# Attention and gated feed-forward in one kernel: values of four heads in a row, products begun block by block, one transpose step moved ahead of the first tile, and another pace of attention beside tile 0

## The chip, the cores and the metric

The kernel runs on one core of a Trainium2 chip. The metric is the device time of one execution in microseconds (us); several executions are timed and the median is given. One execution was also taken with the hardware profiler, and all durations below come from it.

## What is computed

There are 8 batches of 8 heads with 576 positions and 64 numbers per head. Each head gets causal attention with a decay bias; the heads of a batch, side by side, are the rows of a matrix with 4608 rows and 512 columns; a gated feed-forward follows.

```python
scores = q @ k.T / sqrt(64)
cum    = cumsum(max(s, 0))
scores = where(causal, -1e9, scores + min(-(cum_i - cum_j), 0))
x      = softmax(scores) @ v            # 8 x 8 heads -> 4608 x 512
g      = x @ w_gate                     # 512 -> 1536
out    = (g * sigmoid(g) * (x @ w_val)) @ w_out
```

## The kernel before, in words

**Attention.** Heads are numbered 0 to 63 over all batches; four heads make a group, `hb` 0 to 15. For each group, k and q are loaded as float32 (`load_one`, L140), cast to bfloat16 (`cast_one`, L246) and turned so that the head's 64 numbers lie along the partitions. For the first groups TensorE does the turning: `prep_one(hb, i)` issues 5 or 4 transposes into a PSUM bank (`pe_transpose`, L287) for one part of k or q (i = 0 and 2 are the two parts of k, 1 and 3 those of q), then copies the bank's upper half into the tile `kq` at once and leaves the copy of the lower half in a list, `seconds` (`pe_out`, L314 on ScalarE, L316 on VectorE). From group 5 on it goes through memory: the cast tile is stored (`scratch`, L260, `ks` and `qs`), read back by a DMA transpose (`transposes`, L270, `pk` and `pq`) and copied into `kq` by VectorE (`split`, L274).

A head's scores are computed in four chunks (`score_piece`): products into a bank (L359; heads 0 to 7 add a mask by a product, L353), the exponential on ScalarE into the tile `pt` (L369), and for later heads the causal mask on GpSimd (L374, L379). `av_piece` multiplies by the values (15 products with 65 columns, L396), `av_out` divides on VectorE (L412, L413, tile `ot`). For the first two batches, `x_pe` turns a pair of heads by five transposes (L446) and copies them into `XT`, the input of the feed-forward (L451 on ScalarE, L453 on VectorE); later pairs go through memory.

**Feed-forward.** It works on nine tiles of 512 rows. `gate_value` goes over 12 blocks of 128 columns; each block has a gate item and a value item of four products with 512 columns (`products`, L631, one product for each of the four pairs of heads in a batch). The gate is followed by a tanh on ScalarE (L645, `th`) and a VectorE operation (L647, `pp`), the value by another (L658, `ht`). Tiles 0 and 1 then take `down_plain` (L681): 48 products, in tile 0 sorted so that four banks stay open. The other tiles use `down_seven` (L730).

**The order.** All instructions stand in the order in which the code issues them, engine by engine. PSUM has eight banks; `take` hands out the one that was given back longest ago in this order, so that a bank's next user waits for its last reader on the chip.

The heads 0 to 7 come first, in a prologue written out by hand. Before the loop over tiles it begins the first three gate products of tile 0 with three of their four blocks, which need the first three pairs of heads:

```python
        values(4)
        x_pe(0, nc.vector)
        values(5)
        x_pe(1, nc.vector)
        values(6)
        x_pe(2, nc.scalar)
        prep_one(2, 0)
```

In the loop, each item of the feed-forward (`ffn_items`) has a cost `n` in units of one gate or value item. Behind each item, the copies in `seconds` are issued, then what `hook` holds for that `n` (for tile 0: the other three `prep_one` of group 2, the casts of group 3, the loads of `w_out`), and then `pump` issues attention pieces up to a position that grows evenly with `n`: tile 0 takes the attention from position 8.0 (head 8) to 17.65, beginning at n = 5 and ending at n = 36; gate and value end at n = 24. `PREP_AT` puts the turning of group 3 between pieces of heads 8 to 11, `side` and `side_v` put casts, stores and loads beside others: the cast of k 5 on GpSimd stands behind the second score chunk of head 15. `do_later` issues the `split` copies.

**Queues.** Loads of the first q, k and v and all transposes by DMA are issued on SP's queue, the weights and the loads of groups 1 to 3 on GpSimd's queue, in the order of the code. "k 2" and "q 2" below are k and q of group 2.

Of the kernel before, what the change touches and what calls it, by code (L numbers as in the profile page):

```python
# [19 lines left out]
def kernel(  # L20
# [11 lines left out]
    nc = tc.nc  # L32
# [13 lines left out]
    TT = 512  # L46
# [53 lines left out]
    XT = const.tile([128, 4, XR], BF16)  # L100
# [9 lines left out]
    with tc.manual_schedule():  # L110
# [9 lines left out]
        def take():  # L120
            b = min(bank, key=lambda x: released[x])
            assert released[b] < OPEN
            released[b] = OPEN
            return b
# [11 lines left out]
        def load_one(hb, name, rs=(0, NR), eng=nc.sync):  # L136
            b, g = divmod(hb, 2)
            if rs[0] == 0:
                loaded[name, hb] = raw.tile([128, NR, J, D], FP32, tag="raw" + name, name="raw" + name)
            eng.dma_start(  # L140
                loaded[name, hb][:, rs[0] : rs[1], :, :].rearrange("x r j d -> x r (j d)"),
                SRC[name][0][b, g * HB + 2 * rs[0] : g * HB + 2 * rs[1], :, :].rearrange(
                    "(r e) (p j) d -> (e p) r (j d)", e=2, j=J
                ),
            )
# [16 lines left out]
        def cast_v(b, c, eng):  # L162
            n = 128 if c < 4 else TAIL
            dst, src_t = VT[b % 2][0:n, c, :, 0:D], loaded["v", b][0:n, c, :, :]
            if eng is nc.scalar:
                nc.scalar.copy(dst, src_t)
            else:
                eng.tensor_copy(dst, src_t)
# [152 lines left out]
        def w_load(kind, j, h=None):  # L321
            dst = {"g": WG, "v": WV, "o": WO}[kind][j]
            if kind == "o":
                src_ap = moe_w_out[j * WKO * 128 : (j + 1) * WKO * 128, :].rearrange(
                    "(c p) n -> p c n", p=128
                )
            else:
                w = moe_w_gate if kind == "g" else moe_w_val
                lo, hi = (0, WCH) if h is None else (h * WCH // 2, (h + 1) * WCH // 2)
                src_ap = w[:, j * WCH + lo : j * WCH + hi].rearrange("(c p) n -> p c n", p=128)  # L330
                dst = dst[:, :, lo:hi]
            nc.gpsimd.dma_start(dst, src_ap)
# [106 lines left out]
        def x_pe(pr, eng=None):  # L439
            b, r = divmod(pr, H // 2)  # L440
            ot = ots.pop(pr)
            bs = take()
            ps = view16(bs, S)
            for c in range(NCH):
                n = 128 if c < 4 else TAIL
                nc.tensor.transpose(  # L446
                    ps[:, c * 128 : c * 128 + n], ot[0:n, c, :], ident[0:n, 0:n]
                )
            for lo, hi, at in x_parts(b):
                if eng is nc.scalar:  # L450
                    nc.scalar.copy(XT[:, r, at : at + hi - lo], ps[:, lo:hi])  # L451
                else:
                    nc.vector.tensor_copy(XT[:, r, at : at + hi - lo], ps[:, lo:hi])  # L453
            give(bs)
# [69 lines left out]

        seconds = []

        def prep_one(hb, i):
            g, nm = divmod(i, 2)
            nm = ("k", "q")[nm]
            pe_transpose(hb, nm, g)  # L530
            eng = nc.scalar if nm == "k" else nc.vector
            pe_out(hb, nm, g, 0, eng)
            seconds.append(lambda: pe_out(hb, nm, g, 1, eng))

# [12 lines left out]
        def attn_items():  # L547
            for kk in range(H, BH + 2):
                h, step = divmod(kk, HB)
                if kk < BH:  # L550
                    if step == 0:
                        do_later(NR * 2)
                    if step == 1 and 3 < h + 1 < NPE:
                        cast_one(h + 1, "k", nc.gpsimd)
                        cast_one(h + 1, "q", nc.gpsimd)
                    if step == 2 and 3 < h + 1 < NPE:
                        aug(h + 1, GP4)
                    for ci in range(4):
                        score_piece(kk, ci)
                        side(h, step, ci)  # L560
                        side_v(h, step, ci)
                        yield kk + 0.1 + ci / 8
                        if (step, ci) in PREP_AT.get(h, ()):
                            prep_one(h + 1, PREP_AT[h][step, ci])
                            yield kk + 0.1 + ci / 8
                for x in X_AT.get(kk, (kk - 2,)):
                    if x % 2 == 1 and H <= x < BH:
                        if x < XB * H:
                            x_pe(x // 2)
                            yield kk + 0.5  # L570
                        else:
                            x_in(x // 2)
                for p in AV_AT.get(kk, (kk - 1,)):
                    if H <= p < BH:
                        av_piece(p, (0, 1, 2))
                        yield kk + 0.6
                        av_piece(p, (3,))
                        yield kk + 0.7
                        av_piece(p, (4,))
                        av_out(p)  # L580
                        if p >= XB * H and p % 2 == 1:
                            x_out(p // 2)
                        yield kk + 0.8
# [35 lines left out]

        begun = {}  # L620

        def products(kind, ft, xt, cs=range(4)):
            j, f0 = divmod(ft * 128, WCH)
            w = (WG if kind == "g" else WV)[j]
            if (kind, ft) in begun:
                bs, c0 = begun.pop((kind, ft))
                cs = range(c0, 4)
            else:
                bs = take()
            for c in cs:  # L630
                nc.tensor.matmul(  # L631
                    view(bs, TT), w[:, c, f0 : f0 + 128], xt[:, c, :],
                    start=(c == 0), stop=(c == 3),
                )
            if cs[-1] < 3:
                begun[kind, ft] = bs, cs[-1] + 1
            return bs

        def gate_value(tt, hps, sus):
# [255 lines left out]
        def values(*hs):  # L895
            for h in hs:
                av_piece(h, range(NCH))
                av_out(h)
# [20 lines left out]
            cast_v(0, c, nc.gpsimd)  # L919
        load_one(2, "k", eng=nc.gpsimd)  # L920
        cast_v(0, 3, nc.gpsimd)
        w_load("v", 0, 0)
        load_one(2, "q", eng=nc.gpsimd)
        w_load("v", 0, 1)
        for nm in ("g", "v"):
            w_load(nm, 1, 0)
# [25 lines left out]
        load_v(1, range(5))  # L952
        load_qk(4)
        load_qk(5)
        values(4)
        x_pe(0, nc.vector)
        values(5)
        x_pe(1, nc.vector)
        values(6)
        x_pe(2, nc.scalar)  # L960
        prep_one(2, 0)
        while seconds:
            seconds.pop(0)()
        values(7)
        products("g", 0, XT[:, :, 0:TT], range(3))
        x_pe(3, nc.vector)
        for ft in (1, 2):
            products("g", ft, XT[:, :, 0:TT], range(3))
        give(spare)
        first_sbuf.close()  # L970
        PTP[0] = ctx.enter_context(tc.tile_pool(name="later", bufs=1))
# [4 lines left out]
        def pump(upto):  # L976
            while state["pos"] < upto:
                try:
                    state["pos"] = next(at)
                except StopIteration:  # L980
                    state["pos"] = 1e9
# [6 lines left out]
        def at_item(n, f, *args):  # L988
            hook[n].append(lambda: f(*args))

        for n, i in ((1, 2), (2, 1), (3, 3)):
            at_item(n, prep_one, 2, i)
        at_item(7, cast_one, 3, "k", nc.gpsimd)
        at_item(8, cast_one, 3, "q", nc.gpsimd)
        at_item(10, w_load, "o", 0)
# [1 line left out]
        for tt in range(NTT):  # L997
            lo = H * (tt + 1) + LAGS[tt]
            hi = min(H * (tt + 2) + LAGS[tt + 1], BH + 2)
            span = 36 if tt < FIRST7 else 34.5  # L1000
            if hi == BH + 2:
                span = 30
            n0 = 5 if tt == 0 else 0
            n = 0
            todo = {FIRST7 - 1: W_SUMS, FIRST7: W_DIFFS}.get(tt, [])
            if tt == FIRST7:
                for _ in range(3):
                    weight_op(*todo.pop(0))
            for i, cost in enumerate(ffn_items(tt)):
                n += cost  # L1010
                if todo and (i >= 24 if tt < FIRST7 else i % 2 == 1):
                    weight_op(*todo.pop(0))
                if i >= 2 * NFT or i % (2 if tt == 1 else 4) == 1:
                    do_later(1)
                while seconds:
                    seconds.pop(0)()
                for f in hook.pop(n, ()):
                    f()
                pump(lo + (hi - lo) * min(1.0, max(0, n - n0) / (span - n0)))
        pump(1e9)  # L1020


# [28 lines left out]
```

## Time and profile before

| what | value |
|---|---|
| median of 5 runs | 378.45 us (377.62 to 379.64) |
| the profiled execution | 377.62 us |
| its span, first to last instruction | 375.3 us |
| granted TensorE clock, mean | 1.000 |
| TensorE busy | 365.4 us, 97% |
| VectorE, ScalarE, GpSimd busy | 77%, 64%, 57% |
| DMA | 64.23 MB, 171 GB/s on average |

A line of the timeline gives the start, the busy time, engine, code line, operation, output<-input with the shape and the number of instructions merged into it; in brackets, how long the engine was idle just before and what ended that. A line of the chain gives start, length, engine and code line. TensorE's instructions overlap, so their busy times may not be added; the starts tell when the next could go. Times in the text count from the start of the span.

### The profile page before, as it was taken

How to read it: one execution, taken by the hardware profiler on the slowest of the kernel's cores; microseconds unless marked ns; L12 is line 12 of the kernel's file. 1: busy time of each engine (PE TensorE's matmuls, PEld its weight loads, DVE VectorE, ACT ScalarE, POOL GpSimd, SP SyncE). 2: the span in 40 equal slices, each digit the busy share in tenths (PEclk: the TensorE clock that was granted, in tenths of full speed). 3: DMA queues.
4: the chain of work that ended last, by engine and by line, in shares of the span. 5: the costliest groups of instructions: out<-in, count | busy, mean ns of one | idle time of the engine just before them, and what ended most of it. 6: DMA issues, size and time to landing. Idle time of an engine off the chain costs nothing.

```text
span 375.3 us, 8798 instructions
## 1 busy us (share of the span) xinstructions
PE 365.4 (97%) x3300; PEld 231.9 (62%) x3300; DVE 289.9 (77%) x579; ACT 239.9 (64%) x470; POOL 212.9 (57%) x325
## 2 busy tenths in 40 slices
PE   8898999999999999999999999999999999999995
PEld 7574556555555556855685559655865585476464
DVE  7867687367995999679976997599858867975984
ACT  8885967588976887578757876687465523323321
POOL 8965665765465647494649555955675416315320
PEclk9999999999999999999999999999999999999999
DMA  7899999899599997896769775996132103002003
GB/s 238 190 260 254 218 269 263 204 324 243 162 187 276 249 255 216 168 277 216 215 157 262 190 173 166 233 199 152 39 109 73 35 19 128 2 0 90 24 0 114
DMA packets 97146, 64.23 MB, mean 171 GB/s; under 512 B 77232, under 2 KB 82736, under 8 KB 97104
## 3 DMA queue, kind: packets, MB, share of 16 engines
q1 hardware_dynamic: 84976, 41.46, 47.0%
q0 software_dynamic: 12128, 22.21, 22.5%
q8 instruction: 26, 0.43, 0.5%
q14 instruction: 16, 0.13, 0.1%
HBM read 37.90 MB, written 19.86 MB: 154 GB/s over the span
## 4 chain that ended last, share of the span: by engine, by line
PE 87%; DMA 3%; DVE 3%; POOL 2%; ACT 2%; issue 1%; DVEq 0%; POOLq 0%; ACTq 0%
PE bank L631 47%; PE bank L730 17%; PE bank L359 10%; PE bank L396 8%; PE bank L681 3%; DMA pk<-ks 2%; ACT pt L369 1%; DVE kq L316 1%; DMA kq<-HL 1%; DVE pp L647 1%; DMA ks<-ck 1%; DVE ht L658 1%; PE bank L446 1%; PE bank L353 1%; PE bank L287 1%
## 5 line engine op out<-in xcount | busy, mean ns | idle before, releaser
L369 ACT ACTIVATE pt<-bank 128x512 bf16<-128x512 f32 (+1 forms) x256 | 120.2, 509 | 30.9 <-PE bank L359 22.6
L631 PE MATMUL bank<-XT,wv 128*128 128x512 bf16 x432 | 110.9, 379 | 0.6 <-DVE ht L658 0.4
L631 PE MATMUL bank<-XT,wg 128*128 128x512 bf16 x432 | 111.2, 379 | 0.1
L645 ACT ACTIVATE th<-bank 128x512 bf16<-128x512 f32 x108 | 64.7, 599 | 57.9 <-PE bank L631 52.7
L647 DVE SCALAR_TENSOR_TENSOR pp<-th,bank 128x512 bf16<-128x512 bf16 x108 | 73.7, 683 | 21.3 <-ACT th L645 20.8
L658 DVE SCALAR_TENSOR_TENSOR ht<-pp,bank 128x512 bf16<-128x512 bf16 x108 | 74.1, 686 | 10.5 <-PE bank L631 0.4
L359 PE MATMUL bank<-kq 128*128 128x128 bf16 (+4 forms) x576 | 75.3, 240 | 2.0 <-DVE kq L316 1.4
L667 POOL TENSOR_TENSOR ht<-ht 128x512 bf16<-128x512 bf16 x35 | 40.4, 1155 | 52.3 <-DVE su L665 52.2
L359 PEld LDWEIGHTS <-kq 128*128 128x128 bf16 x576 | 45.8, 98 | 32.6 <-issue 3.5
L631 PEld LDWEIGHTS <-wv 128*128 128x128 bf16 x432 | 38.4, 98 | 36.5 <-issue 1.3
L631 PEld LDWEIGHTS <-wg 128*128 128x128 bf16 x432 | 38.3, 98 | 34.1
L374 POOL TENSOR_SCALAR_AFFINE_SELECT pt<-pt 128x512 bf16<-128x512 bf16 x56 | 36.8, 658 | 27.9 <-ACT pt L369 23.0
L396 PEld LDWEIGHTS <-pt 128*128 128x128 bf16 x960 | 41.5, 98 | 16.8
L396 PE MATMUL bank<-vt,pt 128*128 128x65 bf16 x960 | 46.6, 194 | 0.0
L430 POOL DMA_DIRECT2D xs<-ot x24 | 21.7, 904 | 29.6 <-DVE ot L413 27.3
L730 PEld LDWEIGHTS <-ht 128*128 128x128 bf16 x336 | 31.2, 98 | 4.3
L413 DVE TENSOR_TENSOR ot<-bank,rc 128x320 bf16<-128x320 f32 x64 | 31.5, 492 | 2.2
L183 POOL DMA_DIRECT2D kq<-HL x48 | 28.9, 604 | 0.0
L681 PE MATMUL bank<-wo,ht 128*128 128x512 bf16 x96 | 25.8, 379 | 0.0
L730 PEld LDWEIGHTS <-su 128*128 128x128 bf16 x252 | 23.6, 98 | 3.3
L795 POOL TENSOR_TENSOR ysb<-ysb 128x512 f32<-128x512 f32 x12 | 15.2, 1270 | 15.3 <-DVE ysb L789 15.3
L379 POOL TENSOR_SCALAR_AFFINE_SELECT pt<-pt 128x64 bf16<-128x64 bf16 x56 | 14.8, 264 | 14.8 <-ACT pt L369 14.7
(93 smaller groups left out, 388.7 us busy)
## 6 DMA issues: line engine op xcount, KB each, us to landing
out_dram<-ysb POOLq DMA_DIRECT2D x32, 256.0 KB, 4.3
rawv<-in_v_dram SPq DMA_DIRECT2D x28, 256.0 KB
rawk<-in_k_dram SPq DMA_DIRECT2D x12, 576.0 KB
rawq<-in_q_dram SPq DMA_DIRECT2D x12, 576.0 KB
xs<-ot POOLq DMA_DIRECT2D x24, 160.0 KB, 3.7
ks<-ck SPq DMA_DIRECT2D x11, 288.0 KB
qs<-cq SPq DMA_DIRECT2D x11, 288.0 KB
rawk<-in_k_dram POOLq DMA_DIRECT2D x3, 576.0 KB, 7.4
```

The costliest lines, as they stand in the source:

```text
L359: nc.tensor.matmul(sc[:, o : o + w], T[:, 1, e * S + 128 * tj : e * S + 128 * (tj + 1)], T[:, 0, e * S + lo : e * S + hi], start=not maske ...
L369: nc.scalar.activation(pt[:, c0 : c0 + n], sc, AF.Exp, scale=0.125)
L374: nc.gpsimd.affine_select(pt[:, 1088:1600], pt[:, 1088:1600], pattern=[[0, 4], [1, 128]], compare_op=ALU.is_ge, fill=zreg, base=0, channel ...
L396: nc.tensor.matmul(av[:, bi * (D + 1) : (bi + 1) * (D + 1)], pt[:, c0 : c0 + 128], VT[b % 2][:, tj, h, :], start=(tj == 0), stop=(tj == bi),)
L413: nc.vector.tensor_mul(ot[:, :, e * D : (e + 1) * D], av3[:, :, 0:D], rc[:, :, None].to_broadcast([128, NCH, D]),)
L631: nc.tensor.matmul(view(bs, TT), w[:, c, f0 : f0 + 128], xt[:, c, :], start=(c == 0), stop=(c == 3),)
L645: nc.scalar.activation(th, pg, AF.Tanh, scale=0.5)
L647: nc.vector.scalar_tensor_tensor(pp, in0=th, scalar=1.0, in1=pg, op0=ALU.add, op1=ALU.mult)
L658: nc.vector.scalar_tensor_tensor(hp[:, 2 * k2 : 2 * k2 + 2, :].rearrange("p a n -> p (a n)"), in0=pp, scalar=0.5, in1=pv, op0=ALU.mult, op ...
L667: (nc.vector if ft == NFT - 1 else nc.gpsimd).tensor_sub(hp[:, 1:3, :], hp[:, 1:4:2, :], hp[:, 0:3:2, :])
L681: nc.tensor.matmul(view(pys[ts_], DM), hps[ft // 2][:, 2 * (ft % 2) + half, c0 : c0 + 128], WO[j][:, ft % WKO, :], start=(ft == 0), stop=( ...
L730: nc.tensor.matmul(ps, lhs(p), rhs(p), start=(first and p == 0), stop=(last and p == NP - 1), skip_group_check=True,)
```

## The change

- In the prologue, the values of heads 4 and 5, and of heads 6 and 7, come in pairs, each `x_pe` stands one step later, and the copy of `x_pe(1)` goes from VectorE to ScalarE.
- The first three gate products are begun with two blocks each, spread around `x_pe(2)` and `x_pe(3)`; their third blocks follow behind the transposes of k 2. `products` is split into `block`, `begin` and `products` for this.
- Both parts of q 2 are turned in the prologue, in front of the first item (`prep_one(2, 1)` and `(2, 3)`); the second part of k 2 moves from item 1 to item 2. The load of q 2 is issued ahead of the first half of `wv` instead of behind it.
- For group 3 the copies of the first parts of k and q go to ScalarE and those of the second parts to VectorE, where k had gone to ScalarE and q to VectorE.
- Behind an item, one copy of `seconds` is issued, where all were.
- In tile 0, the attention reaches 0.52 of its way at n = 24 and the rest by n = 36; it had been 0.61 at n = 24.

```diff
-        def prep_one(hb, i):
+        def prep_one(hb, i, eng=None):
             g, nm = divmod(i, 2)
             nm = ("k", "q")[nm]
             pe_transpose(hb, nm, g)
-            eng = nc.scalar if nm == "k" else nc.vector
+            if eng is None:
+                eng = nc.scalar if nm == "k" else nc.vector
...
-                            prep_one(h + 1, PREP_AT[h][step, ci])
+                            prep_one(
+                                h + 1, PREP_AT[h][step, ci],
+                                (nc.scalar, nc.vector)[ci // 2] if h == 2 else None,
+                            )
...
-        def products(kind, ft, xt, cs=range(4)):
+        def block(kind, ft, xt, bs, cs):
...
+        def begin(kind, ft, cs):
+            bs = begun.pop((kind, ft))[0] if (kind, ft) in begun else take()
+            block(kind, ft, XT[:, :, 0:TT], bs, cs)
+            begun[kind, ft] = bs, cs[-1] + 1
+
+        def products(kind, ft, xt):
+            bs, c0 = begun.pop((kind, ft)) if (kind, ft) in begun else (take(), 0)
+            block(kind, ft, xt, bs, range(c0, 4))
             return bs
...
+        load_one(2, "q", eng=nc.gpsimd)
         w_load("v", 0, 0)
-        load_one(2, "q", eng=nc.gpsimd)
         w_load("v", 0, 1)
...
-        values(4)
         x_pe(0, nc.vector)
-        values(5)
-        x_pe(1, nc.vector)
-        values(6)
+        values(4, 5)
+        x_pe(1, nc.scalar)
+        values(6, 7)
+        begin("g", 0, range(2))
         x_pe(2, nc.scalar)
+        begin("g", 1, range(2))
+        begin("g", 2, range(2))
+        x_pe(3, nc.vector)
         prep_one(2, 0)
         while seconds:
             seconds.pop(0)()
-        values(7)
-        products("g", 0, XT[:, :, 0:TT], range(3))
-        x_pe(3, nc.vector)
-        for ft in (1, 2):
-            products("g", ft, XT[:, :, 0:TT], range(3))
+        for ft in range(3):
+            begin("g", ft, range(2, 3))
+        for i in (1, 3):
+            prep_one(2, i)
...
-        for n, i in ((1, 2), (2, 1), (3, 3)):
-            at_item(n, prep_one, 2, i)
+        at_item(2, prep_one, 2, 2)
...
-                while seconds:
+                if seconds:
                     seconds.pop(0)()
...
-                pump(lo + (hi - lo) * min(1.0, max(0, n - n0) / (span - n0)))
+                done = min(1.0, max(0, n - n0) / (span - n0))
+                if tt == 0:
+                    done = (
+                        0.52 * max(0, n - n0) / (24 - n0) if n < 24
+                        else min(1.0, 0.52 + 0.48 * (n - 24) / (span - 24))
+                    )
+                pump(lo + (hi - lo) * done)
```

More of the change, by code (lines that the diff above doesn't have):

```diff
@@ L620 @@
         begun = {}
-        def products(kind, ft, xt, cs=range(4)):
+        def block(kind, ft, xt, bs, cs):
             j, f0 = divmod(ft * 128, WCH)
             w = (WG if kind == "g" else WV)[j]
[L625 to L629, printed above, removed]
             for c in cs:
@@ L634, in products @@
                 )
-            if cs[-1] < 3:
-                begun[kind, ft] = bs, cs[-1] + 1
+        def begin(kind, ft, cs):
[5 more added lines that the diff above has]
+            block(kind, ft, xt, bs, range(c0, 4))
             return bs
```

## The prediction

> **What bounds the kernel.** I read the page first. TensorE is busy for 97% of the span and has 87% of the chain, so only its idle time and the order around it can move the end. The slices (9.4 us each) show the DMA engines full from the second to the eighth, to about 75 us.
>
> ```profile
> PE 365.4 (97%) x3300; PEld 231.9 (62%) x3300; DVE 289.9 (77%) x579; ACT 239.9 (64%) x470; POOL 212.9 (57%) x325
> ...
> DMA  7899999899599997896769775996132103002003
> ```
>
> Next TensorE's timeline. A busy bar overlaps the next, so I count by starts: four 512-wide products take 0.86 us (0.216 each), five transposes of `prep_one` 0.28, `x_pe` 0.45, one head's values 0.46, a score chunk 0.22.
>
> ```profile
> 28.04 0.53 PE L446 MATMUL bank<-ident,ot 128*128 128x128 bf16 x5 [0.17 <-DVE ot L413]
> ...
> 32.91 1.03 PE L631 MATMUL bank<-XT,wv 128*128 128x512 bf16 x4
> 35.30 0.82 PE L359 MATMUL bank<-kq 128*128 128x128 bf16 x8 [1.37 <-DVE kq L316]
> ...
> 45.66 1.02 PE L631 MATMUL bank<-XT,wv 128*128 128x512 bf16 x4 [0.38 <-DVE ht L658]
> ```
>
> The products of 32.91 are issued by 33.77 and the first score chunk of head 8 starts at 35.30: 1.53 lost, to VectorE's copies of q 2. By the same count TensorE loses 0.21 at 25.85, 0.33 at 28.04, 0.27 at 37.35, 0.20 at 44.86, 0.55 at 45.66 and 0.24 at 47.84. Sum 3.33 us. After that it runs without a stop but for one place, which the chain in order of time shows:
>
> ```profile
> 64.51 0.61 PE bank L396 x20
> 65.12 0.24 PE bank L359 x4
> ...
> 65.44 0.61 ACT pt L369
> ...
> 66.10 0.63 POOL pt L374
> 66.73 1.10 POOL ck L246
> ...
> 67.85 3.13 DMA ks<-ck
> ...
> 71.00 5.73 DMA pk<-ks
> ...
> 76.75 0.22 DVE kq L274
> 76.97 0.57 issue
> 77.55 0.45 DVE XT L453
> 77.99 0.04 issue
> 78.03 1.24 PE bank L631 x5
> ```
>
> This is not a TensorE chain: head 15's first score chunk (64.95 in the timeline) releases its exponential, its mask, then k 5's cast behind it on GpSimd, its store, its DMA transpose, `split` on VectorE, and queued behind `split` the copy of `x_pe(7)`, which the first gate product of tile 1 needs in its fourth step. From 64.95 to 78.03 it takes 13.08 us. TensorE waits there 0.31 us, so the two are nearly level.
>
> GpSimd's timeline shows the loads that come last in front of that:
>
> ```profile
> 24.83 1.14 POOL L246 CAST ck<-rawk 128x1152 bf16<-128x1152 f32 x1 [1.50 <-DMA rawk<-in_k_dram]
> 28.46 1.15 POOL L246 CAST cq<-rawq 128x1152 bf16<-128x1152 f32 x1 [2.49 <-DMA rawq<-in_q_dram]
> ...
> 37.76 1.13 POOL L246 CAST ck<-rawk 128x1152 bf16<-128x1152 f32 x1 [0.26 <-DMA rawk<-in_k_dram]
> ```
>
> **Load of q 2.** Its issue (0.70) moves past one `wv` half's (0.77) on GpSimd. k 2 landed at 24.7, the `wv` half at 18.90+7.7=26.6, q 2 at 19.66+8.7=28.3 (issue plus time to landing). Swapped, q 2 needs its own 1.7 behind k 2 and lands at 26.4, the `wv` half at 28.3. q 2's cast then ends near 27.6. The `wv` half is first used at 29.93 (below): 1.6 of cover, and each us beyond it would stop TensorE for a us. What is queued ahead of k 3 is the same, so k 3 still lands just before 37.76 and its cast ends at 38.89.
>
> **Prologue, after.** No instruction is added on TensorE. From 23.36 (head 7's scores done): `x_pe(0)` 0.45, values 4, 5 0.92, `x_pe(1)` 0.45, values 6, 7 0.92: 26.09. Two blocks of g0 0.43, `x_pe(2)` 0.45, four blocks 0.86, `x_pe(3)` 0.45: 28.28. Its input is head 7's `ot`: values end 26.25, then reciprocal and product on VectorE, 27.16, so under cover. Five k 2 transposes 0.28, three blocks 0.65, nine q 2 transposes 0.50: 29.71. Then g0 to v2 with the last k 2 transposes 3.46: 33.17. The gaps of 0.21 and 0.33 are filled. `x_pe(1)`'s copy goes from VectorE (0.45) to ScalarE (0.64), which is idle at 25.4. `seconds` now gives one copy per item; k 2's last one (0.72, ScalarE) then ends at 33.05, and only head 10 reads it.
>
> VectorE now has q 2's four copies (0.81, 0.72 each twice) from 29.65, mixed with pp and ht (0.69 each, 0.79 apart where ht waits for its pp): q 31.1, pp0 31.75, q 32.49, ht0 33.09, q 33.72, pp1 34.33, ht1 35.12, pp2 35.73, ht2 36.52. The whole queue started at 30.85 before, and the score chunk had to wait for the third q copy. Now all that it reads is done by 32.5, so the 1.53 goes. What is late next is banks: chunk 3 takes the bank of q's last copy (0.16 lost at 33.61), g3 that of pp1 (0.39), v3 that of pp2 (0.29). TensorE would be at k 3's transposes at 38.37, but the cast ends at 38.89: 0.55 lost. Together 1.39, and no step up to here can go below that while k 3 lands where it does.
>
> **Between 39 and 65.** For k 3 and q 3 the copies are split by halves: two k copies (0.72) go to VectorE, two q copies (0.74) to ScalarE; and fewer scores lie in gate/value. Following both queues with the rows' durations, the banks come free 0.2 to 1.5 us before they are taken (g7 takes at 44.52 a bank free at 44.30, head 10's second chunk at 42.97 one free at 42.44, g8 at 46.5 one free at 45.7). The 0.20, 0.55 and 0.24 go. Upper bound: all three stay, 0.99. I take nothing, since VectorE has 2.58 us idle before 44.12 even now. Saved in all: 3.33-1.39=1.94.
>
> **The pace.** The built order says what the new pace costs: 36 of tile 0's 48 down products stood behind head 15's first chunk, now 27. Nothing else between it and tile 1 differs. So the chunk stands 9 x 0.216=1.94 later in TensorE's queue. Its time is 64.95-1.94+1.94, by my ledger 64.87. The 13.08 us behind it hold the same instructions in the same order on GpSimd, SP and VectorE, so the copy of `x_pe(7)` ends near 77.95 and tile 1's first product goes on there. TensorE arrives at 75.5 and now waits 2.4 us where it waited 0.31. From there on its queue is that of before, so the whole saving is given back. Even an earlier chunk helps little: the store of k 5 stands in SP's queue behind k 6 and q 6 (issued 63.17 and 63.82), with the DMA engines full. `ks` took 3.13 here and 2.56 at 103.17, so at most 0.6 is to be had.
>
> The down projection's start moves from 60.0 to 55.7; the first `wo` half lands at 40.93+10.9=51.8, the second at 44.26+16.1=60.4, used at 66.4: covered.
>
> **Clock.** The longest idle of TensorE after its start is that 1.53, in a window with the full clock:
>
> ```profile
> 32.00:36.00 4.00, 2.63 (x18) 1.35 (x17) 3.91 (x7) 1.37 (x3) 0.62 (x2) 1.00 1.22 264
> ```
>
> No row shows what 2.4 us of idle does to it; I charge nothing. [...]
>
> **Sum.** The profiled run took 377.62, its span 375.3, so 2.32 lie outside; the median of five is 0.83 above it. -0.08 at the chain gives 375.2, 377.5, and in terms of the median 378.3. A measurement of this kernel tells about 0.3% (1.1 us) from no change.
>
> **Rivals.** Faster: the transpose lands early. `pk` took 5.73 us, the largest single piece, with only 1.31 of issue on SP; were it about 3.5, TensorE's own work would set tile 1 and 1.94+0.31 would show: 376.2. For it: the front's gain is sure, the DMA time is one sample. Against: VectorE's 2.65 us wait on it, and the store ahead of it that is held by the queue.
> Slower: the front fails to pay for the pace. Head 15's chunk is 1.94 later in the order whatever the front does; if only 0.5 is saved (the 0.99 stays and banks on VectorE cost 0.45 more), the chunk is 1.44 late and so are cast, store and end: 379.9. It decides when less than 0.8 is saved. For it: VectorE is busy 3.91 of 4 us at 32 to 36. Against: the queue in front of the store swallows the first 0.5.
> No effect: q 2 lands at 28.3 as before. Then its cast ends at 29.6 and TensorE waits 0.4 at 29.2, which the wait for k 3 swallows: 378.3.
>
> **Chances.** Forecast 0.60 and no effect 0.04: own range 377.4 to 379.1 (ends: `ks` 0.6 shorter and a little off `pk`; up to 0.8 of new bank waits), of which 0.53 lie within 0.3%, 0.08 below, 0.03 above. Faster rival 0.19, slower rival 0.17. So 0.27 faster, 0.53 same, 0.20 slower. The range reaches into both rivals: 376.5 to 379.7.
>
> **What would show it.** Right: the gap before head 8's first chunk gone; a short wait at k 3's transposes near 38.9; head 15's chunk near 64.9; a wait of about 2.4 us in tile 1's first gate product, on VectorE's `XT` copy behind `split`. Wrong: `split` done before 76, or TensorE waiting on banks between 39 and 65.

## The result: slower by 0.4%, by a clock that the forecast charged nothing

The changed kernel takes 379.19 us (median of 41 runs, 377.28 to 383.53) against 377.82 us (78 runs) for the kernel before. The ratio is 1.0038, with a 95% interval of 1.0028 to 1.0049. The forecast was 378.3 us and "the same". It stood on before's median of five runs, 378.45; as differences, -0.1 us was forecast and +1.4 measured. The profiled execution took 379.1 us with a span of 377.3, where before had 377.62 and 375.3: 2.0 us more.

The page of the changed kernel, busy time and slices. The granted clock had been full in before's profile. Code lines are counted in each kernel's own file, so the gate and value products stand at L630 or L631, `pp` at L647 or L653, `ht` at L658 or L664:

```profile
span 377.3 us, 8799 instructions
...
PE 365.5 (97%) x3300; PEld 231.5 (61%) x3300; DVE 291.5 (77%) x578; ACT 240.8 (64%) x471; POOL 212.2 (56%) x325
...
PEclk9999999989999999999999999999999999999999
```

TensorE's busy time is the same within 0.1 us, but one slice, from 75.5 to 84.9 us, has a clock of 8. That slice holds the start of tile 1.

First the front, in TensorE's timeline:

```profile
33.44 0.61 PE L359 MATMUL bank<-kq 128*128 128x128 bf16 x6
34.36 0.38 PE L359 MATMUL bank<-kq 128*128 128x320 bf16 x2 [0.32 <-DVE kq L316]
35.08 1.02 PE L630 MATMUL bank<-XT,wg 128*128 128x512 bf16 x4 [0.34 <-DVE pp L653]
...
39.05 0.44 PE L287 MATMUL bank<-ident,ck 128*128 128x128 bf16 x5
```

The wait in front of head 8's first chunk is gone; the chunk starts at 33.44 instead of 35.30. Counted by starts, as in the forecast, there are 0.48 in front of its third chunk (34.36), 0.50 in front of g3 (35.08) and 0.28 in front of v3 (36.47). The transposes of k 3 (39.05) do not wait, and from there to tile 1 no gap is left. The loads, in GpSimd's timeline:

```profile
25.82 1.15 POOL L246 CAST cq<-rawq 128x1152 bf16<-128x1152 f32 x1 [0.27 <-DMA rawq<-in_q_dram]
37.24 1.13 POOL L246 CAST ck<-rawk 128x1152 bf16<-128x1152 f32 x1 [1.61 <-DVE ht L664]
```

q 2's cast ends at 26.97 (it was 29.61), and k 3's at 38.37. Then the chain to tile 1, in order of time:

```profile
65.50 0.61 ACT pt L369
...
66.80 1.09 POOL ck L246
...
67.92 3.30 DMA ks<-ck
...
71.23 4.84 DMA pk<-ks
...
76.13 1.73 issue
77.87 0.45 DVE XT L453
...
78.36 1.24 PE bank L630 x5
```

Head 15's exponential starts at 65.50 (65.44 before), the fourth step of tile 1's first gate product at 78.36 (78.03 before). All of the front's gain is given back there, 0.33 more with it, as a wait of TensorE, which its timeline shows in brackets:

```profile
75.21 0.81 PE L630 MATMUL bank<-XT,wg 128*128 128x512 bf16 x3
78.36 0.38 PE L630 MATMUL bank<-XT,wg 128*128 128x512 bf16 x1 [2.33 <-DVE XT L453]
```

And right behind that wait, by windows (window, length, busy time of the five engines, then the granted clock, DMA share, GB/s):

```profile
79.00:80.00 1.00, 1.00 (x6) 0.50 (x5) 0.60 (x1) 0.37 (x1) 0.77 (x2) 0.74 1.00 394
80.00:83.00 3.00, 3.00 (x16) 1.44 (x14) 1.85 (x4) 1.84 (x4) 0.00 (x0) 0.52 1.10 368
```

The clock is 0.74 for 1 us and 0.52 for 3: 0.26 + 3 x 0.48 = 1.70 us of TensorE's time lost. By half microseconds it is 0.99 up to 79.5, 0.50 in each of the six from there to 82.5, 0.60 in the next and 1.00 from 83.0 on: about 3.4 us at half clock. In before's profile the same windows have 1.00:

```profile
79.00:80.00 1.00, 1.00 (x8) 0.44 (x6) 0.51 (x1) 0.93 (x2) 0.99 (x3) 1.00 1.02 387
80.00:83.00 3.00, 3.00 (x41) 1.89 (x40) 2.73 (x6) 2.49 (x6) 1.28 (x4) 1.00 1.01 376
```

0.33 + 1.70 = 2.03 is the whole difference of the spans. From the fourth step to the end of the span it takes 297.3 us in before and 298.9 in the changed kernel.

It is not in every execution. Of the 41 runs, 22 have a mean clock of 0.996 or less, and their median is 380.2 us; the other 19 have a median of 378.3. Only the profiled execution shows where in the run the clock was low.

### The profile page after: what moved, and what is told of

It is laid out like the page before. It is cut to its first block, busy times and chain, and to the rows that moved or that the text cites. A ratio compares the mean times of both kernels' runs of the same rounds, so it can differ in the third digit from the quotient of the medians.

```text
span 377.3 us, 8799 instructions
## 1 busy us (share of the span) xinstructions
PE 365.5 (97%) x3300; PEld 231.5 (61%) x3300; DVE 291.5 (77%) x578; ACT 240.8 (64%) x471; POOL 212.2 (56%) x325
## 4 chain that ended last, share of the span: by engine, by line
PE 90%; DMA 3%; DVE 2%; ACT 2%; issue 1%; POOL 0%; SPq 0%; DVEq 0%; ACTq 0%
PE bank L630 49%; PE bank L736 17%; PE bank L359 10%; PE bank L396 8%; PE bank L687 4%; DMA pk<-ks 1%; DVE kq L316 1%; ACT pt L369 1%; DMA rawq<-in_q_dram 1%; DMA ks<-ck 1%; PE bank L287 1%; PE bank L353 1%; PE bank L446 1%; DVE pp L653 0%; DVE ht L664 0%
## 5 line engine op out<-in xcount | busy, mean ns | idle before, releaser
L630 PE MATMUL bank<-XT,wg 128*128 128x512 bf16 x432 | 112.4, 381 | 2.7 <-DVE XT L453 2.3
L630 PE MATMUL bank<-XT,wv 128*128 128x512 bf16 x432 | 111.1, 380 | 0.1
L653 DVE SCALAR_TENSOR_TENSOR pp<-th,bank 128x512 bf16<-128x512 bf16 x108 | 73.8, 683 | 19.7 <-ACT th L651 18.9
L664 DVE SCALAR_TENSOR_TENSOR ht<-pp,bank 128x512 bf16<-128x512 bf16 x108 | 74.1, 686 | 10.8 <-PE bank L630 0.6
L359 PE MATMUL bank<-kq 128*128 128x128 bf16 (+4 forms) x576 | 76.1, 241 | 0.5 <-DVE kq L316 0.3
L630 PEld LDWEIGHTS <-wv 128*128 128x128 bf16 x432 | 38.5, 98 | 38.5 <-issue 3.1
L630 PEld LDWEIGHTS <-wg 128*128 128x128 bf16 x432 | 38.5, 98 | 34.8 <-issue 1.3
```

The lines of the kernel that those rows point to most:

```text
L359: nc.tensor.matmul(sc[:, o : o + w], T[:, 1, e * S + 128 * tj : e * S + 128 * (tj + 1)], T[:, 0, e * S + lo : e * S + hi], start=not maske ...
L630: nc.tensor.matmul(view(bs, TT), w[:, c, f0 : f0 + 128], xt[:, c, :], start=(c == 0), stop=(c == 3),)
L653: nc.vector.scalar_tensor_tensor(pp, in0=th, scalar=1.0, in1=pg, op0=ALU.add, op1=ALU.mult)
L664: nc.vector.scalar_tensor_tensor(hp[:, 2 * k2 : 2 * k2 + 2, :].rearrange("p a n -> p (a n)"), in0=pp, scalar=0.5, in1=pv, op0=ALU.mult, op ...
```

## The experiments

Theory A: the new pace puts head 15's chunk back to where it was, TensorE then waits 2.3 us in tile 1's first gate product, and this wait brings the clock of 0.50 for 3.4 us in the profiled execution and the lower mean clock in 22 of 41 runs. The rivals: the wait alone is the loss; the pace is harmless; or what sets the end there is not the chain of DMAs but something beside it. The whole front lies earlier or later from one profile to the next: k 5's cast starts at 66.75 in the changed kernel and at 68.79 in the one with 8 fills, which has the same instructions up to there. So times in different profiles are compared from one instruction to another, not from the span's start.

### Fill the wait

`ident` products into a bank that nobody reads stand ahead of the fourth step of tile 1's first gate product (40 here, 8 and 16 in two later kernels).

```diff
+            if FILL and kind == "g" and ft == 0:
+                block(kind, ft, xt, bs, range(c0, 3))
+                n = FILL.pop()
+                other = min(bank, key=lambda x: released[x])
+                for _ in range(n):
+                    nc.tensor.matmul(view(other, 128), ident, ident, start=True, stop=True)
+                c0 = 3
             block(kind, ft, xt, bs, range(c0, 4))
...
+            if tt == 1:
+                FILL.append(40)
```

> The changed kernel with 40 products of 128x128 (2.2 us, into a bank that nobody reads) put in front of the fourth block of tile 1's first gate product, where TensorE waited 2.50 us. Theory A (the wait is fixed by the transpose's chain, and it is the half clock behind the wait that makes the kernel slower): the wait is filled, nothing ends later, no record of half clock, mean clock 1.000, and the time falls from 1.004 of the kernel before to 1.000 to 1.001 (about 378.0 us). Theory B (the kernel is slower because head 15's chunk and what hangs on it stand later; the clock is a side show of one execution): the time stays near 1.004 (379.2 us). Theory C (new waits for banks in tile 0): stays near 1.004 as well.

```profile
76.41 2.40 PE L648 MATMUL bank<-ident 128*128 128x128 bf16 x40
78.90 0.38 PE L631 MATMUL bank<-XT,wg 128*128 128x512 bf16 x1
```

That is TensorE's timeline with 40 fills. The fourth step stands as late behind the first as in the changed kernel (75.76 to 78.90, there 75.21 to 78.36), but TensorE is idle for only 0.26 by starts. The clock is above 0.996 in all 12 runs; 377.92 us, where the runs of before beside it have 377.56, ratio to before 0.9994 (0.997 to 1.0017). So the lower clock here hangs on the idle time: with the same front and the same lateness it does not come. The lateness keeps its own small price. The span is 376.2, 0.9 above before's, and the fourth step is 0.87 later than before's; behind it there are 297.3 us again, as in before, where the changed kernel has 298.9. The 1.6 to 1.7 us between them are the clock's.

### How much idle time it takes

> The kernel after, with 16 small products of 128 columns into an unread bank ahead of the fourth block of tile 1's first gate product, so that TensorE's wait of 2.5 us shrinks to about 1.6. [...] Theory A2 (any wait above 1 us there can do it): clocks under 0.996 in about as many runs as in the kernel after, ratio near 1.004.

> The kernel after with 8 small products ahead of the fourth block of tile 1's first gate product: TensorE's wait about 2.0 us, between e6_fill16 (1.45 us, one run of 12 under a clock of 0.996) and the kernel after (2.33 us, about half of its runs). [...] If there is a sharp bound below 2 us: about half or more of them, ratio near 1.004; if it lies above 2 us: none or one, 1.000 to 1.001.

With 16 fills:

```profile
78.37 0.38 PE L631 MATMUL bank<-XT,wg 128*128 128x512 bf16 x1 [1.45 <-DVE XT L453]
```

With 8:

```profile
80.41 0.38 PE L631 MATMUL bank<-XT,wg 128*128 128x512 bf16 x1 [1.90 <-DVE XT L453]
```

With 16 fills the wait shown is 1.45 us: one run of 12 has a clock of 0.996 or less, 377.87 us, ratio 0.9999 (0.9985 to 1.0013). With 8 the wait is 1.90: two of 12, 378.47 us, ratio 1.0004 (0.9975 to 1.0033). With 2.33 it is 22 of 41. The kernel before, beside all these, has it in 6 of 87 runs. So up to 1.9 us it is hardly more than what happens anyway, and at 2.33 about every second execution pays. A bound near 2 us fits, and so does a chance that rises with the length of the wait; the counts are too small to tell them apart.

### Take the copy out of VectorE's queue

```diff
-                            x_pe(x // 2)
+                            x_pe(x // 2, nc.scalar if x == 2 * H - 1 else None)
```

> The changed kernel with the last copy of tile 1's input, that of x_pe(7), on ScalarE instead of VectorE, where it stood behind split and its wait for the DMA transpose. Theory A: no wait at tile 1's first gate product; its fourth block goes on near 75.9 instead of 78.4, the clock stays full, and the front's saving of 1.94 us shows with the 0.31 that the kernel before lost there: ratio to before 0.994 (375.6 us). If the transpose's chain is waited for somewhere else (split's result in head 20's scores, or pp behind split on VectorE), part of it comes back there: 0.996 to 0.999. Theories B and C: 1.002 to 1.004, since the later chunk and the banks are as they were.

> The kernel before with the same copy on ScalarE. Theory A: only the 0.31 us of its own wait there goes: ratio 0.999, hardly to be told from 1.000. If the copy's engine were worth something by itself, it would be well below that, 0.995 like the changed kernel with the same edit.

In the changed kernel with this edit, `split` on VectorE, the copy on ScalarE and TensorE's four steps are:

```profile
75.49 3.31 DVE L274 COPY kq<-pk 64x1152 bf16<-64x1152 bf16 x1 [1.81 <-DMA pk<-ks]
```

```profile
76.24 0.68 ACT L451 COPY XT<-bank 128x576 bf16<-128x576 bf16 x1
```

```profile
76.07 1.27 PE L630 MATMUL bank<-XT,wg 128*128 128x512 bf16 x4
```

`split` takes 3.31 us and nobody waits for it; the four steps go in one piece, with 0.25 lost. 376.24 us, ratio 0.9952 (0.9925 to 0.998): faster than both kernels. The same edit in before gives 0.9993 (0.9971 to 1.0015), nothing. So the change's gain was real, and one copy's place in a queue held it back.

### The pace, with and without the copy in the way

> The changed kernel with the pace of before in tile 0 (0.61 of the attention at n = 24), so head 15's first chunk stands 1.94 us earlier in TensorE's queue, and all else of the change stays. If head 15's chunk sets the transpose's chain (as my prediction's ledger had it): cast of k 5 near 64.8, its store and transpose 1.9 us earlier, tile 1 begins near 76.1, ratio 0.995. If the DMA queue sets it (the store waits behind k 6 and q 6, which land near 70 whatever TensorE does): transpose still lands near 76, tile 1's fourth block near 77.5, TensorE waits 1 to 1.8 us and the clock rarely drops: ratio 0.998 to 1.000.

> The kernel before with nothing but the new pace (0.52 at n = 24). Theory A (the pace puts head 15's first score chunk 1.94 us later in TensorE's queue, the wait in tile 1's first gate product grows, and the wait halves the clock in part of the runs): the gaps in front of 39 us stay (2.34 in sum), those of 44.9 to 47.9 (0.99) go or stay, the chunk comes 0.95 to 1.94 later than before's 64.95, the XT copy 1 to 2 later (79 to 80), TensorE waits 2 to 2.5 there; ratio to before 1.003 to 1.007, the profiled clock under 1.000 in part of the runs. Theory B (the pace costs nothing by itself, the slowdown needs the other edits): ratio 0.997 to 1.001.

> The kernel after with the old pace, and with the copy of x_pe(7) on ScalarE, which does not stand behind split. Tells what the new pace is worth where the copy is not in the way. If it only brings the wait at tile 1 (front and gaps between 39 and 65 the same without it): as e2_xt_act, ratio 0.995 to 0.997. If the old pace brings back waits on banks and on k 3's cast between 36 and 48 (1 to 2 us in e4_old_pace): 0.997 to 1.000, with 0.3 less than e4_old_pace.

The edits take out, or put into before, the five lines of `done` for `tt == 0`. Ratios to before, with 95% intervals:

| | old pace | new pace |
|---|---|---|
| before's front | 1 | 1.0095 (1.0074 to 1.0116) |
| new front | 0.9985 (0.9959 to 1.0011) | 1.0038 (1.0028 to 1.0049) |
| new front, copy on ScalarE | 1.001 (0.9989 to 1.0031) | 0.9952 (0.9925 to 0.998) |

With the copy behind `split`, the new pace makes the kernel slower, with either front. On the old one it costs more than I expected: k 5's cast starts at 70.44 instead of 66.68. The front is 0.40 late in that profile, the later place costs 1.94 that no saved time pays for, k 3's transposes wait 0.99 and three places between 48 and 53 lose another 1.40 by starts, where before lost 0.99 between 44 and 48. Then comes the same wait:

```profile
82.05 0.38 PE L631 MATMUL bank<-XT,wg 128*128 128x512 bf16 x1 [2.34 <-DVE XT L453]
```

Four of its six runs have the lower clock, the profiled one does not (1.00 in the 6 us behind the wait). There the lateness alone is the loss: the fourth step is 4.02 us later than in before and the span 4.0 longer. With the copy on ScalarE the new pace makes the kernel faster, and the two intervals do not meet. Why it helps there shows in the new front with the old pace:

```profile
39.18 0.45 PE L287 MATMUL bank<-ident,ck 128*128 128x128 bf16 x5 [1.09 <-POOL ck L246]
```

The old pace puts the transposes of k 3 0.85 us earlier in TensorE's queue (measured from head 8's third chunk, the wait taken off), and there they wait for k 3's cast: 1.26 by starts, 0.50 for a bank behind it. So k 5's cast starts only 0.33 us earlier than in the changed kernel. The ratio of that run lies in the range of my second case, but by another mechanism: the wait of 1 to 1.8 us at tile 1 that the case asked for is not there (0.31 by starts, as in before). What I had left out was that the pace moves k 3's transposes as well. With the copy on ScalarE and the old pace the same wait is 2.02 us, and the ratio is a little above what I gave; the two runs with the old pace cannot be told apart.

### What holds `split`

`split` took 0.45 to 0.96 us over the 22 copies of `pk` in before; 0.87 in before's chain, 1.84 in the changed kernel's. GpSimd's timeline at that point, in the changed kernel, and VectorE's:

```profile
74.88 1.72 POOL L168 CAST vt<-rawv 128x512 bf16<-128x512 f32 x3
76.56 0.23 POOL L379 TENSOR_SCALAR_AFFINE_SELECT pt<-pt 128x64 bf16<-128x64 bf16 x1
76.74 0.60 POOL L168 CAST vt<-rawv 128x512 bf16<-128x512 f32 x1
77.30 0.77 POOL L708 DMA_DIRECT2D out_dram<-ysb  x1
```

```profile
76.10 1.84 DVE L274 COPY kq<-pk 64x1152 bf16<-64x1152 bf16 x1 [3.28 <-DMA pk<-ks]
```

In before, the casts come in another order, with a DMA issue between the first and the next two:

```profile
75.50 0.60 POOL L168 CAST vt<-rawv 128x512 bf16<-128x512 f32 x1
76.05 0.58 POOL L702 DMA_DIRECT2D out_dram<-ysb  x1
76.64 1.45 POOL L168 CAST vt<-rawv 128x512 bf16<-128x512 f32 x2
```

```profile
76.75 0.87 DVE L274 COPY kq<-pk 64x1152 bf16<-64x1152 bf16 x1 [2.65 <-DMA pk<-ks]
```

There `split` is done at 77.62, while these casts still run, and one of the casts took 0.90 instead of 0.60. All four kernels with the old pace have this order and a `split` of 0.71 to 0.92.

In the changed kernel `split` starts in the middle of a string of casts and ends at 77.94, 0.6 behind the string's end (77.34), beside a DMA issue that takes 0.77 instead of the 0.56 to 0.61 of others there. In all kernels with the new pace and the casts on GpSimd it ends there, wherever it started: it takes 1.82 to 3.31 us. To try it, the casts of v for batch 2 go to ScalarE:

```diff
-                cast_v(2, V2_AT[step, ci], nc.gpsimd)
+                cast_v(2, V2_AT[step, ci], nc.scalar)
```

> The kernel after, with the casts of the third group of v (those beside the split of k 5) on ScalarE instead of GpSimd. Theory C (the split copy on VectorE took 1.84 us here, 0.87 in before, because GpSimd's casts run beside it): split 0.5 to 0.9, the XT copy about 1 us earlier (near 76.9), TensorE's wait about 1.3, few clock drops, ratio to before 0.999 to 1.001. Rival (split's time has nothing to do with GpSimd): split stays at 1.5 to 3, the wait at 2 to 2.5, ratio near 1.004.

```profile
77.90 0.45 DVE L274 COPY kq<-pk 64x1152 bf16<-64x1152 bf16 x1 [2.63 <-DMA pk<-ks]
78.28 0.44 DVE L453 COPY XT<-bank 128x576 bf16<-128x576 bf16 x1
```

`split` takes 0.45, TensorE's wait is 0.29, and from the cast of k 5 to the copy it takes 9.07 us instead of 11.12. So GpSimd's casts held it. One engine stood still beside the other: `split` lasted up to 3.31 us instead of 0.45, and in before one of the casts 0.90 instead of 0.60. In the kernels with the new pace `split` stood through several casts in a row; by what means, and what decides who goes first, no run shows. The time is no better, 379.08 us, ratio 1.0035 (1.0019 to 1.005): the chain has ScalarE's exponentials, casts and tanh in one string from 77.87 to 82.47 ahead of a `pp`, and TensorE loses 0.71, 0.45 and 0.45 us by starts to late `pp` and `ot` up to 88.2. Two of its 12 runs have a clock of 0.996 or less, so the clock's loss was mostly gone, and waits like these took its place. That part of my expectation fell.

In this profile the front waits 2.19 us for the first loads, which the changed kernel's did not (0.16 at the same place, 10.61), and the clock is 0.83 between 10 and 20 us:

```profile
12.38 0.83 PE L359 MATMUL bank<-kq 128*128 128x128 bf16 x8 [2.19 <-DMA kq<-HL]
```

```profile
10.00:20.00 10.00, 7.07 (x62) 5.12 (x62) 7.34 (x10) 5.98 (x15) 9.38 (x13) 0.83 0.83 183
```

10 x 0.17 = 1.7 us are lost, as much as at tile 1 in the changed kernel, in the 10 us that hold another wait over 2 us. Not every such wait comes with a lower clock: behind the 2.02 us at k 3's transposes in the kernel with the old pace and the copy on ScalarE, the clock is 1.00 (39 to 45).

### The load of q 2

> The kernel after with q 2's load behind the first half of wv again, as in before. By the prediction's step q 2's cast ends near 28.5 to 29.6 instead of 27.0, TensorE waits 0 to 0.5 us at q 2's transposes near 29.2, and the chain behind head 15's chunk moves by no more: ratio to before 1.002 to 1.006, as the kernel after. Rival (the swap carries the front's gain): head 8's first chunk is over 1 us later than in the kernel after and the ratio is above 1.006.

With the load issued behind the `wv` half again, q 2's cast ends at 30.85 in a front that is 1 us late, and TensorE waits 0.41 by starts at its transposes (0.25 shown). 379.33 us, ratio 1.0042 (1.0016 to 1.0068), as the changed kernel. The swap is worth the few tenths given. They are not swallowed, as the prediction had it, by the wait for k 3, since there is none: k 5's cast starts 1.44 later than in the changed kernel, the late front and the 0.41 together. The medians cannot tell so little. This profile has the 2.33 us wait at tile 1 as well, but no lower clock behind it (1.00 from 79 to 86), and 6 of its 10 runs have a mean of 0.996 or less: the same wait, by chance with and without.

## Why the forecast was wrong, by its own steps

**Front: right.** q 2's cast ends at 26.97 (forecast 27.6), k 2's and q 2's transposes go without a wait, and the gap of 1.53 is gone. Ahead of head 8's third chunk, g3 and v3 the banks cost 1.26 instead of 0.84. k 3's cast ended 0.5 earlier than I took and TensorE came 0.7 later, so the 0.55 at its transposes did not occur: 1.26 in all where I had 1.39.

**Between 39 and 65: right.** The gaps of 0.20, 0.55 and 0.24 are gone, though with the old pace a wait of 0.50 for a bank comes back there, so the pace has a part in it.

**Pace: right in size.** The chain starts at 65.50 where -0.08 from 65.44 was forecast (the front of this profile is 0.2 late), TensorE arrives at the fourth step near 75.9, and waits 2.50 by starts where I had 2.4. I had not seen that the pace also takes k 3's transposes out of a wait.

**Chain: right to 0.3, by the wrong hold.** I took its 13.08 us as a sum of cast, store, transposes and `split`. In the changed kernel the DMAs were 0.72 us faster and `split` 0.97 longer, so that the sum came out is luck. "The same instructions in the same order" did not hold on GpSimd: with the new pace the DMA issue stands ahead of the casts of v and no longer between them. The length is set by GpSimd: between the start of k 5's cast and the copy of `x_pe(7)` it is 11.11 to 11.13 us in six profiles with the new pace and the copy on VectorE (changed kernel, pace alone, 8, 16 and 40 fills, old place of q 2's load), while the two DMAs together take from 6.9 to 8.2. For the same reason an early `pk`, the faster rival, did not help: in the kernel with the pace alone the two DMAs took 6.92 instead of 8.86, and `split` gave it back with 3.06.

**Clock: the step that failed.** "No row shows what 2.4 us of idle does to it; I charge nothing." The term was put at nothing because no row had a price; it should have had two ends, nothing and a stretch at a lower clock. It cost 1.70 us in the profiled execution, and 1.9 in the median of the runs with a lower clock against the others (380.2 and 378.3). In the profiled execution 2.33 us of idle came with it, and 22 of the 41 runs have the lower mean clock; what decides which of them do, no run shows. Without the lower clock the runs have a median of 378.3, 0.45 above before; 0.33 of that is the fourth step.

**The slower rival** had the right sign by another mechanism: the front did pay for the pace.

## What to carry to other kernels

Here a wait of TensorE of 2.33 us was no free place to put saved time: in the profiled execution about 3.4 us at a clock of 0.50 followed, 1.7 us lost, and 22 of 41 runs have a lower mean clock. When work is moved so that TensorE arrives earlier at a fixed point, look for what stands in front of the awaited copy in its engine's queue; here one copy moved to ScalarE turned a loss of 0.4% into a gain of 0.5%. The chain that ended here on a VectorE copy beside GpSimd's casts took 11.11 to 11.13 us in six profiles, whether its two DMAs took 6.9 us or 8.2, and 9.07 with the casts on ScalarE; look whether a change has put the casts in one unbroken string.

## What was not expected of the hardware

TensorE's clock was 0.50 for about 3.4 us (79.5 to 82.9), from 1.1 us behind the end of an idle time of 2.33 us; 22 of 41 runs of that kernel have a lower mean clock, and 1 of 12 where the idle time is 1.45 us. A VectorE copy that took 0.45 us with the casts on ScalarE lasted 3.31 us beside four GpSimd casts, and in the changed kernel's chain most of such a copy (1.73 of 1.84 us) stands as "issue".
